# Where one Tanh stands in ScalarE's order, in a soft-capped attention fused with a spectral token mixer

## The chip, the core and the metric

The kernel runs on one core of a Trainium2 chip. The core has a TensorE (matmul, in the profile PE, with its weight loads PEld), a VectorE (DVE), a ScalarE (ACT), a GpSimd (POOL) and a SyncE (SP), which here issues nearly all DMAs. Each engine executes its own instructions in the order in which they were written for it, and waits on semaphores for the others. The metric is device time in microseconds (us) of one execution; of a kernel with several runs, the median.

## The reference

Batch 8, 12 heads, sequence 448, head size 64, model width 768. All in float32.

```python
def _attn_ref(q, k, v, cap):
    scores = np.matmul(q, k.transpose(0, 1, 3, 2)) / np.sqrt(q.shape[-1])
    scores = cap * np.tanh(scores / cap)
    scores = scores - np.max(scores, axis=-1, keepdims=True)
    attn = np.exp(scores)
    attn = attn / (np.sum(attn, axis=-1, keepdims=True) + 1e-09)
    return np.matmul(attn, v)

def _moe_ref(x, w_theta, w_tok_r, w_tok_i, w_ch):
    theta = x @ w_theta
    zr, zi = x * np.cos(theta), x * np.sin(theta)
    y = np.einsum('ts,bsd->btd', w_tok_r, zr) + np.einsum('ts,bsd->btd', w_tok_i, zi)
    u = x + y
    return u + np.maximum(u @ w_ch, 0.0)
```

The attention's output, with its heads side by side, is the `x` of the second function.

## The kernel before

Heads are worked in pairs: 8 batches of 6 pairs, 48 pairs in all. Activations lie transposed, with features in the partitions. float32 products whose accuracy matters are made of three matmuls on operands that are split into a rounded high part and a low remainder (`zh` and `zl`, `hi` and `lo`, `wtk_h` and `wtk_l`): high by high, high by low, low by high.

The function `pipeline` writes one slot after the other. Slot `s` makes the scores of pair `s` and, one slot late, the attention output of pair `k = s - 1`; from slot 8 on (FIRST) it also holds one sixth of the second function for batch `b`, called its part: `b, part = divmod(s - 8, 6)`. There are 56 slots, and slots from 48 on have no scores (`live` is false). What an engine does in which order is set by the order in which this Python code writes the instructions; no scheduler moves them.

A slot writes, in this order: the first half of the scores (`qk_half(s, 0)`: matmuls of line 217 into the PSUM tile `s`, then a Tanh of line 219 from there into the tile `p`); the attention output (`av`, line 257, and its copy `x` on ScalarE, line 260); the sums of the exponentials (`sums`, line 273, into the PSUM tile `r`); the second half of the scores with its Tanh (`qk_half(s, 1)`); then the list of steps of its part (`part_scripts`). In that list "A" and "B" stand for the Exp of the first and second half (line 225), "a" and "b" for partial sums of the exponentials on VectorE (lines 247 and 250).

The steps that this document speaks of:
- `transp(b, j)` (lines 355 to 357): seven transposes on TensorE of feature block `j` into two PSUM tiles `t`, four and three blocks. For each of the two, ScalarE rounds it to `zh` (line 356) and VectorE subtracts to get `zl` (line 357).
- `mix(b, j)` (lines 364 to 367): 21 matmuls of `zh` and `zl` with the token weights into a PSUM tile `mx`, then an addition to `x` on VectorE.
- `sincos` (lines 341 and 342): two Sin passes on ScalarE, with a table load ahead; the next Exp needs another load.
- `rotate` (line 346): x times sine and cosine, on VectorE.
- `invert` (line 296): the reciprocal `ri` of the sums `r` on VectorE, and four DMAs on SyncE that spread it to `bc`. It is written for odd `k` only.
- `prep(s + 1)` (lines 193 and 194): the split of the next pair's q and k on VectorE, from slot 13 on, and a DMA for the pair behind.

Part 2 of each batch is the slot whose list begins with a transposition, `(transp, 1)`; 1 is the feature block, the first one having been transposed at the end of part 1. Its list is transp 1, sincos 1, mix 0, rotate 3, transp 2, "A", mix 1, "a", rotate 4, transp 3, "B", mix 2, "b", rotate 5. Parts 2 with scores are slots 10, 16, 22, 28, 34, 40 and 46. In them `invert` and `prep` are written right behind the first entry, so VectorE takes the reciprocal after the two subtractions of transp 1.

PSUM has two pools. `psS` holds one tile `s`, which both halves of the scores use in turn. `psM` holds four tiles, shared by `a`, `r`, `t`, `th`, `mx` and `ch`: a new one takes the buffer that was released first in program order.

Of the kernel before, what the change touches and what calls it, by code (L numbers as in the profile page):

```python
# [16 lines left out]
AF = mybir.ActivationFunctionType  # L17
# [15 lines left out]
WHOLE = 14  # L33
# [3 lines left out]
def softcap_attn_then_spectral_mix(ctx, tc, qk2, v, cap, w_theta, w_tok, w_ch, ident, outT):  # L37
    nc = tc.nc
    B, NP, P, _, S = qk2.shape
    D = P // 2  # L40
    CP = v.shape[2]
# [4 lines left out]
    NS = B * NP  # L46
# [14 lines left out]
    qscale = const.tile([P, 1], F32, name="qscale")  # L61
# [20 lines left out]
    def fill(n):  # L82

        t = psM.tile([P, 512], F32, tag="m", name=f"fill{len(fills)}")
        fills.append(t)
        for _ in range(n):
            nc.tensor.matmul(t[:32, :CP], ones_sb, ones_sb[:, :1].broadcast_to([CP, CP]), start=True, stop=True)
# [77 lines left out]
    def weights(s, pos):  # L165
        for word in WEIGHTS.get((s, pos), "").split():
            step = steps[word[-3:-1], int(word[-1])]
            {">": step.load, "*": step.scale, "#": step.vscale}.get(word[0], step.split)()
# [8 lines left out]
    def load_qk(k):  # L177

        if 0 < k < WHOLE:
            raw[k] = wk.tile([P, 2, S], F32, tag=("hi", "lo")[k % 2], name=f"qk{k}", bufs=1)  # L180
        else:
            raw[k] = qk_sb
        nc.sync.dma_start(raw[k], qk2[k // NP, k % NP])

    def load_v(k):
        vt[k] = wk.tile([CP, 2, NCH, D], F32, tag="v", name=f"v{k}", bufs=2)
        nc.sync.dma_start(vt[k], v[k // NP, k % NP])
# [10 lines left out]
    def apart(k):  # L198


        return k < NP and k % 2 == 0

    def qk_half(k, half):

        sp = psS.tile([P, 2, 2, 512], F32, tag="s", name=f"s{k}_{half}")
        if apart(k):
            pp = wk.tile([CP, 2, 2, S], F32, tag="xhl", name=f"p{k}_{half}", bufs=3)
        else:
            pp = wk.tile([CP, 2, 2, S], F32, tag="p", name=f"p{k}_{half}", bufs=3)
        pt[k, half] = pp  # L210
        for i in range(2):
            ks = slice((2 * half + i) * CP, (2 * half + i + 1) * CP)
            products = ((raw, raw),) if k < WHOLE else ((hi, hi), (lo, hi), (hi, lo))
            for n, (kk, qq) in enumerate(products):
                for hh in range(2):
                    rows = slice(hh * D, (hh + 1) * D)
                    nc.tensor.matmul(sp[:CP, i, hh, :S], kk[k][rows, 1, ks], qq[k][rows, 0, :],  # L217
                                     start=n == 0, stop=n == len(products) - 1)
        nc.scalar.activation(pp, sp[:CP, :, :, :S], AF.Tanh, scale=qscale[:CP])  # L219

    def exp_half(k, half):

        pp = pt[k, half]
        if not state["general"]:
            nc.scalar.activation(pp, pp, AF.Exp, scale=cap_sb[:CP])  # L225
        elif half:
            first = pt[k, 0]
            mx = wk.tile([CP, 2, S], F32, tag="ps", name=f"mx{k}", bufs=2)
            am = wk.tile([CP, 2, S], F32, tag="ps", name=f"am{k}", bufs=2)
            nc.vector.tensor_tensor(mx, first[:, 0], first[:, 1], op=ALU.max)  # L230
            nc.vector.tensor_tensor(mx, mx, pp[:, 0], op=ALU.max)
            nc.vector.tensor_tensor(mx, mx, pp[:, 1], op=ALU.max)
            nc.gpsimd.partition_all_reduce(am, mx, CP, bass_isa.ReduceOp.max)
            for t in (first, pp):
                for i in range(2):
                    nc.vector.tensor_tensor(t[:, i], t[:, i], am, op=ALU.subtract)
                nc.scalar.activation(t, t, AF.Exp, scale=cap_sb[:CP])
# [14 lines left out]
    def av(k):  # L252
        va = vt.pop(k)
        acc = psM.tile([P, 512], F32, tag="m", name=f"a{k}")
        for c in range(NCH):
            for hh in range(2):
                nc.tensor.matmul(acc[hh * D : (hh + 1) * D, :S], va[:, hh, c, :], pt[k, c // 2][:, c % 2, hh, :],  # L257
                                 start=c == 0, stop=c == NCH - 1)
        x = wk.tile([P, S], F32, tag="x", name=f"x{k}", bufs=12)
        nc.scalar.copy(x, acc[:, :S])  # L260
        X[k // NP, k % NP] = x
# [13 lines left out]
    def sums(k, halves=(0, 1)):  # L275

        alone = state["general"] or NP <= k < DIRECT
        if not alone and k % 2 == 0:
            return
        if state["general"] and 0 not in halves:  # L280
            return
        if (k % 2 == 0 or not alone) and 0 in halves:
            state["r"] = psM.tile([P, 512], F32, tag="m", name=f"r{k}")
        sum_pairs((k,) if alone else (k - 1, k), state["r"], halves)

    def invert(k):

        if k % 2 == 0:
            return
        r = state.pop("r")  # L290
        ri = wk.tile([P, S], F32, tag="ri", name=f"ri{k}", bufs=1)
        if state["general"]:
            nc.vector.tensor_scalar_add(ri, r[:, :S], 1e-9)
            nc.vector.reciprocal(ri, ri)
        else:
            nc.vector.reciprocal(ri, r[:, :S])  # L296
        for n in (k - 1, k):
            bc[n] = wk.tile([P, S], F32, tag="bc", name=f"bc{n}", bufs=2)
            for i in range(2):
                nc.sync.dma_start(bc[n][i::2, :], ri[D * (n % 2) : D * (n % 2) + D, :])  # L300
# [92 lines left out]
    def us(b, j):  # L393
        split_x(b, j, "us")

    def pipeline(general):
        state["general"] = general
        load_v(0)
        load_qk(1)
        for step in (("tk", 0), ("tk", 1)):  # L400
            steps[step].load()

        for s in range(FIRST + 6 * B):
            k = s - 1
            b, part = divmod(s - FIRST, 6)
            live = s < NS
            start = s < FIRST
            if s == 0:
                fill(FILL["first scores"])
            if live:  # L410
                qk_half(s, 0)
            if s == 0:
                fill(FILL["half"])
            if start:
                weights(s, "a")
                exp_half(s, 0)
            if 0 <= k < NS:
                av(k)
            if not start:
                weights(s, "a")  # L420
            if not start and part == 4:
                for j in range(NJ // 2, NJ):
                    us(b, j)
            if s + 1 < NS:
                load_v(s + 1)
            if 0 <= k < NS:
                sums(k, (0,) if start else (0, 1))
                if not start and part != 2:
                    invert(k)
            if live:  # L430
                qk_half(s, 1)
            if s == 0:
                fill(FILL["slot"])
            if 0 <= k and start:
                sums(k, (1,))
            if s + 2 <= WHOLE:
                load_qk(s + 2)
            if WHOLE <= s + 1 < NS and (start or part != 2):
                prep(s + 1)
            weights(s, "b")  # L440
            if 0 <= k and start:
                invert(k)
            script = ["B", "a", "b"] if start else part_scripts(b)[part]
            for i, e in enumerate(script):
                if not start and i == len(script) - 1:
                    weights(s, "c")
                    if s % 2 == 1 and s <= NS + 1:
                        norm(s - 3)
                        norm(s - 2)
                if isinstance(e, str):  # L450
                    if live:
                        if e in "AB":
                            exp_half(s, "AB".index(e))
                        else:
                            add_half(s, "ab".index(e))
                else:
                    e[0](b, e[1])
                if part == 2 and i == 0 and not start:
                    if 0 <= k < NS:
                        invert(k)  # L460
                    if WHOLE <= s + 1 < NS:
                        prep(s + 1)
            if start:
                weights(s, "c")
                for n in {4: (0, 1), 5: (2, 3), 7: (4, 5)}.get(s, ()):
                    norm(n)
                for j in {6: range(4), 7: range(4, NJ)}.get(s, ()):
                    split_x(0, j, "xs")
# [12 lines left out]
    with arm.Else():  # L481
        with tc.manual_schedule():
            pipeline(general=True)
# [38 lines left out]
```

## Time and profile before

| | |
|---|---|
| median of 3 runs | 964.53 us (964.43 to 966.29) |
| profiled execution | 966.27 us |
| its span, first to last instruction | 964.5 us |
| granted TensorE clock, mean | 0.997 |
| Tanh (line 219), 96 times | 168.7 us, 1757 ns each |
| Exp (line 225), 96 times | 170.6 us, 1790 ns each |
| rounding of transposes (line 356), 96 times | 45.9 us, 534 ns mean of two shapes |
| subtraction (line 357), 96 times | 55.2 us, 616 ns mean of two shapes |
| reciprocal (line 296), 24 times | 70.8 us, 2952 ns each |
| table loads on ScalarE, 30 | 1283 ns each |

In a row of the timeline stand the start in us from the span's start, the duration in us, the engine, the line, the operation, the names (output, then inputs, without buffer numbers), the shapes and a count of instructions drawn together; in brackets the idle time of the engine ahead of it, and what ended it. Waits are inferred from semaphore events. A TensorE row's start is recorded, and its end is modelled.

### The profile page before, as it was taken

To read this page: it belongs to the slowest core of one execution; us is meant where nothing else is said; L and a number is where in the kernel's file an instruction comes from. 1 tells how busy PE (TensorE), PEld (TensorE's weight loads), DVE (VectorE), ACT (ScalarE), POOL (GpSimd) and SP (SyncE) were. 2 spreads that over 40 slices of the span, in tenths; PEclk is the share of its full clock that TensorE was granted. 3 is DMA by queue.
4 is the path that set the end of the run, shared out by engine and by line. 5 is a ranking of instruction groups with operands and counts; after the bars stand their busy time and mean duration, and the time that the engine had idled before them with its cause. 6 is when DMAs were issued, how large, how long until landed. Compare 5 with 4: busy or idle time off the path is not lost.

```text
span 964.5 us, 12776 instructions
## 1 busy us (share of the span) xinstructions
PE 945.6 (98%) x5224; PEld 697.3 (72%) x5224; DVE 640.8 (66%) x877; ACT 590.5 (61%) x609; POOL 0.4 (0%) x6
## 2 busy tenths in 40 slices
PE   8999999999999999999999999999999999999997
PEld 4234766677778777777787687767777877789897
DVE  5998787885855757756766559656585576664541
ACT  6888784667654687546963578456775558722520
POOL 0000000000000000000000000000000000000000
PEclk9999999999999999999999999999999999999999
DMA  7564122330113212132122221033011321001001
GB/s 252 193 194 138 34 82 94 112 103 30 49 39 105 67 39 63 32 98 67 32 66 68 77 67 48 29 87 94 31 49 39 105 68 39 20 15 62 0 1 61
DMA packets 30739, 68.68 MB, mean 71 GB/s; under 512 B 4304, under 2 KB 16720, under 8 KB 30672
## 3 DMA queue, kind: packets, MB, share of 16 engines
q1 hardware_dynamic: 30672, 67.78, 23.0%
q8 instruction: 43, 0.70, 0.3%
q14 instruction: 24, 0.20, 0.1%
HBM read 45.74 MB, written 11.01 MB: 59 GB/s over the span
## 4 chain that ended last, share of the span: by engine, by line
PE 88%; DVE 6%; ACT 4%; issue 1%; POOL 0%; POOLq 0%
PE a L257 15%; PE s L217 14%; PE mx L364 6%; PE mx L366 6%; PE mx L365 6%; PE th L322 6%; PE ch L322 6%; PE ch L324 6%; PE th L323 6%; PE ch L323 6%; PE th L324 6%; PE t L355 3%; PE r L273 3%; ACT p L219 2%; DVE ri L296 2%
## 5 line engine op out<-in xcount | busy, mean ns | idle before, releaser
L219 ACT ACTIVATE p<-s,qscale 112x1792 f32<-112x1792 f32 x96 | 168.7, 1757 | 168.7 <-PE s L217 168.7
L225 ACT ACTIVATE p<-p,cap_sb 112x1792 f32<-112x1792 f32 x96 | 170.6, 1790 | 0.6
L257 PE MATMUL a<-p,v 112*64 112x448 f32 x768 | 154.9, 545 | 0.0
L364 PE MATMUL mx<-wtk_h,zh 128*128 128x448 f32 x336 | 126.8, 377 | 5.4 <-DVE ri L296 3.6
L366 PE MATMUL mx<-wtk_h,zl 128*128 128x448 f32 x336 | 123.6, 368 | 0.0
L365 PE MATMUL mx<-wtk_l,zh 128*128 128x448 f32 x336 | 123.5, 367 | 0.0
L257 PEld LDWEIGHTS a<-p,v 112*64 112x64 f32 x768 | 50.9, 136 | 86.9 <-issue 77.1
L322 PE MATMUL th<-xs,wth_h 128*128 128x448 f32 x288 | 106.9, 371 | 0.0
L322 PE MATMUL ch<-us,wch_h 128*128 128x448 f32 x288 | 106.8, 371 | 0.0
L324 PE MATMUL ch<-us,wch_l 128*128 128x448 f32 x288 | 105.5, 366 | 0.0
L323 PE MATMUL th<-xs,wth_h 128*128 128x448 f32 x288 | 105.4, 366 | 0.0
L323 PE MATMUL ch<-us,wch_h 128*128 128x448 f32 x288 | 105.3, 366 | 0.0
L324 PE MATMUL th<-xs,wth_l 128*128 128x448 f32 x288 | 105.3, 366 | 0.0
L250 DVE TENSOR_TENSOR ps<-ps,p 112x896 f32<-112x896 f32 x80 | 87.0, 1087 | 1.4
L296 DVE RECIPROCAL ri<-r 128x448 f32<-128x448 f32 x24 | 70.8, 2952 | 12.0 <-PE r L273 11.9
L335 DVE SCALAR_TENSOR_TENSOR g_sb<-g_sb 128x448 f32<-128x448 f32 x48 | 29.9, 624 | 65.8 <-ACT g_sb L334 65.4
L364 PEld LDWEIGHTS mx<-wtk_h,zh 128*128 128x128 f32 x336 | 63.6, 189 | 11.9 <-issue 5.0
L357 DVE TENSOR_TENSOR zl<-t,zh 128x512 fp32r<-128x512 f32 x96 | 55.2, 616 | 24.5 <-ACT zh L356 24.5
L375 DVE SCALAR_TENSOR_TENSOR x<-ch,x 128x448 f32<-128x448 f32 x48 | 29.8, 620 | 59.0 <-PE ch L324 59.0
L366 PEld LDWEIGHTS mx<-wtk_h,zl 128*128 128x128 f32 x336 | 63.5, 189 | 5.4
L365 PEld LDWEIGHTS mx<-wtk_l,zh 128*128 128x128 f32 x336 | 63.7, 190 | 4.9
L322 PEld LDWEIGHTS ch<-us,wch_h 128*128 128x128 f32 x288 | 54.1, 188 | 9.6 <-issue 4.6
(75 smaller groups left out, 1377.8 us busy)
## 6 DMA issues: line engine op xcount, KB each, us to landing
qk_sb<-in_qk SPq DMA_DIRECT2D x35, 448.0 KB, 3.4
v<-in_v SPq DMA_DIRECT2D x48, 224.0 KB, 2.5
bc<-ri SPq DMA_DIRECT2D x96, 112.0 KB, 2.3
out_dram<-x SPq DMA_DIRECT2D x48, 224.0 KB, 1.9
qk<-in_qk SPq DMA_DIRECT2D x13, 448.0 KB, 3.4
g_sb<-in_wth SPq DMA_DIRECT2D x6, 768.0 KB, 5.4
g_sb<-in_wch SPq DMA_DIRECT2D x6, 768.0 KB, 4.7
swk_raw<-in_wtok SPq DMA_DIRECT2D x7, 448.0 KB, 4.1
```

The lines of the kernel that those rows point to most:

```text
L217: nc.tensor.matmul(sp[:CP, i, hh, :S], kk[k][rows, 1, ks], qq[k][rows, 0, :], start=n == 0, stop=n == len(products) - 1)
L219: nc.scalar.activation(pp, sp[:CP, :, :, :S], AF.Tanh, scale=qscale[:CP])
L225: nc.scalar.activation(pp, pp, AF.Exp, scale=cap_sb[:CP])
L250: nc.vector.tensor_tensor(pst[k], pst[k], pt[k, 1][:, i], op=ALU.add)
L257: nc.tensor.matmul(acc[hh * D : (hh + 1) * D, :S], va[:, hh, c, :], pt[k, c // 2][:, c % 2, hh, :], start=c == 0, stop=c == NCH - 1)
L296: nc.vector.reciprocal(ri, r[:, :S])
L322: nc.tensor.matmul(acc[:, :S], wh[:, j, ms], t[:, 0, :], start=j == 0, stop=False)
L323: nc.tensor.matmul(acc[:, :S], wh[:, j, ms], t[:, 1, :], start=False, stop=False)
L324: nc.tensor.matmul(acc[:, :S], wl[:, j, ms], t[:, 0, :], start=False, stop=j == NJ - 1)
L364: nc.tensor.matmul(acc[:, :S], zh[:, c, :], wtk_h[:, c, :], start=c == 0, stop=False)
L365: nc.tensor.matmul(acc[:, :S], zh[:, c, :], wtk_l[:, c, :], start=False, stop=False)
L366: nc.tensor.matmul(acc[:, :S], zl[:, c, :], wtk_h[:, c, :], start=False, stop=c == NC2 - 1)
```

## The change

`qk_half` no longer issues its Tanh; it returns a function that does. For the first half, and for the second half of every slot but the parts 2, that function is called at once, so nothing moves there. In the parts 2 (`late`) it is called after the first entry of the list, that is after `transp(b, 1)`, ahead of `invert` and `prep`, which stand where they stood.

```diff
-        nc.scalar.activation(pp, sp[:CP, :, :, :S], AF.Tanh, scale=qscale[:CP])
+        return lambda: nc.scalar.activation(pp, sp[:CP, :, :, :S], AF.Tanh, scale=qscale[:CP])
...
             if live:
-                qk_half(s, 0)
+                qk_half(s, 0)()
...
+            late = not start and part == 2
             if live:
-                qk_half(s, 1)
+                tanh = qk_half(s, 1)
+                if not late:
+                    tanh()
...
-            if WHOLE <= s + 1 < NS and (start or part != 2):
+            if WHOLE <= s + 1 < NS and (not late):
                 prep(s + 1)
...
-                if part == 2 and i == 0 and not start:
+                if late and i == 0:
+                    if live:
+                        tanh()
                     if 0 <= k < NS:
                         invert(k)
                     if WHOLE <= s + 1 < NS:
```

ScalarE's instructions in slot 22 (batch 2), before and after; the number behind a name tells instances apart, `p_1` is the second half of the scores, and `zh_1` the rounding of transp 1:

```order
 L219 ACTIVATE p_0_2664<-s_0_2663,qscale 112x1792
 L260 COPY x_2687<-a_2678 128x448
+L356 CAST zh_1_2710<-t_1_0_2712 128x512
+L356 CAST zh_1_2710<-t_1_4_2719 128x384
 L219 ACTIVATE p_1_2697<-s_1_2696,qscale 112x1792
-L356 CAST zh_1_2711<-t_1_0_2713 128x512
-L356 CAST zh_1_2711<-t_1_4_2720 128x384
 L341 ACT_TABLE_LOAD
 L341 ACTIVATE g_sb_87<-g_sb_87,quarter 128x3x448
```

The two roundings have passed the Tanh; the same happens in the six other slots. No table load is added.

VectorE's instructions at the same place, which are the same in both kernels but for the instance numbers (those of before are shown), with the engines that each waits for:

```order
L357 TENSOR_TENSOR zl_1_2712<-t_1_0_2713,zh_1_2711 128x512 [waits Activation_49]
L357 TENSOR_TENSOR zl_1_2712<-t_1_4_2720,zh_1_2711 128x384 [waits Activation_49]
L296 RECIPROCAL ri_2726<-r_2691 128x448
L193 CAST hi_2734<-qk_sb 128x896 [waits DMAHW7_49]
L194 TENSOR_TENSOR lo_2735<-qk_sb,hi_2734 128x896 [waits DVE_49]
L367 TENSOR_TENSOR x_1359<-mx_0_2741,x_1359 128x448 [waits PE_49]
L346 TENSOR_TENSOR g_sb_87<-g_sb_87,x_1780 128x896 [waits Activation_49]
```

Nothing has moved on VectorE: the reciprocal still stands behind the two subtractions, and these wait for ScalarE.

TensorE's instructions from transp 2 to the start of mix 1 in that slot, again the same in both:

```order
L355 MATMUL t_2_0_2767<-ident_sb,g_sb_86 128x128 [waits DVE_49]
L355 MATMUL t_2_0_2767<-ident_sb,g_sb_86 128x128 x3
L355 MATMUL t_2_4_2774<-ident_sb,g_sb_86 128x128 [waits DVE_49]
L355 MATMUL t_2_4_2774<-ident_sb,g_sb_86 128x128 x2
L364 MATMUL mx_1_2781<-wtk_h,zh_1_2711 128x448 [waits DVE_49,Activation_49]
```

Nothing has moved here either: the first matmul of mix 1 waits for VectorE and for ScalarE.

## The prediction

> **What bounds the kernel now.** I read the page first: busy shares, then the chain that ended last.
>
> ```profile
> PE 945.6 (98%) x5224; PEld 697.3 (72%) x5224; DVE 640.8 (66%) x877; ACT 590.5 (61%) x609; POOL 0.4 (0%) x6
> PE 88%; DVE 6%; ACT 4%; issue 1%; POOL 0%; POOLq 0%
> ```
>
> TensorE is busy 98% of the span and carries 88% of the chain. A reordering on ScalarE can only buy what TensorE waits for. So the next view is the list of TensorE's waits (us in total, times, longest):
>
> ```profile
> PE s L217 <- ACT p L219: 6.7, 7, 1.9
> PE mx L364 <- DVE ri L296: 3.6, 7, 0.5
> ```
>
> The second row matters: seven times a mix matmul (line 364) waits for VectorE's reciprocal `ri`. Seven is the number of slots that the change touches (s = 10, 16, 22, 28, 34, 40, 46), and 3.6/7 = 0.51 us each, with a longest of 0.5, so they are alike. The first row is the second scores' wait for the first half's Tanh, which the change leaves in place. The timeline of slot 22, rows of three engines in order of time (start, duration), shows what stands behind such a wait:
>
> ```profile
> 359.76 0.98 PE L355 MATMUL t<-ident_sb,g_sb 128*128 128x128 f32 x7
> 359.86 1.76 ACT L219 ACTIVATE p<-s,qscale 112x1792 f32<-112x1792 f32 x1 [1.76 <-PE s L217]
> 360.00 1.08 DVE L346 TENSOR_TENSOR g_sb<-g_sb,x 128x896 f32<-128x896 f32 x1
> 361.52 0.95 ACT L356 CAST zh<-t 128x512 fp32r<-128x512 f32 x2
> 362.13 1.16 DVE L357 TENSOR_TENSOR zl<-t,zh 128x512 fp32r<-128x512 f32 x2 [1.05 <-ACT zh L356]
> 362.49 1.28 ACT L341 ACT_TABLE_LOAD   x1
> 363.20 2.94 DVE L296 RECIPROCAL ri<-r 128x448 f32<-128x448 f32 x1
> 364.65 0.37 PE L366 MATMUL mx<-wtk_h,zl 128*128 128x448 f32 x1
> 364.86 0.93 PE L355 MATMUL t<-ident_sb,g_sb 128*128 128x128 f32 x7
> 365.11 1.31 ACT L342 ACTIVATE g_sb<-g_sb 128x1344 f32<-128x1344 f32 x1
> 366.29 0.45 PE L364 MATMUL mx<-wtk_h,zh 128*128 128x448 f32 x1 [0.51 <-DVE ri L296]
> 366.32 0.94 ACT L356 CAST zh<-t 128x512 fp32r<-128x512 f32 x2
> 368.20 1.08 DVE L346 TENSOR_TENSOR g_sb<-g_sb,x 128x896 f32<-128x896 f32 x1
> 368.58 1.80 ACT L225 ACTIVATE p<-p,cap_sb 112x1792 f32<-112x1792 f32 x1
> 369.20 1.15 DVE L357 TENSOR_TENSOR zl<-t,zh 128x512 fp32r<-128x512 f32 x2
> 370.44 0.37 PE L366 MATMUL mx<-wtk_h,zl 128*128 128x448 f32 x1
> 370.65 0.93 PE L355 MATMUL t<-ident_sb,g_sb 128*128 128x128 f32 x7
> 371.29 0.97 ACT L356 CAST zh<-t 128x512 fp32r<-128x512 f32 x2 [0.91 <-PE t L355]
> 371.33 0.45 PE L364 MATMUL mx<-wtk_h,zh 128*128 128x448 f32 x1
> 371.39 1.08 DVE L247 TENSOR_TENSOR ps<-p 112x896 f32<-112x896 f32 x1
> 372.14 1.81 ACT L225 ACTIVATE p<-p,cap_sb 112x1792 f32<-112x1792 f32 x1
> ```
>
> Read backwards: mix 1 starts at 366.29, 0.15 after the reciprocal ends (363.20 + 2.94 = 366.14), because it takes the PSUM buffer that `r` leaves. The reciprocal stands behind the two subtractions `zl` in VectorE's queue. These waited 1.05 us for the rounding `zh` on ScalarE, and `zh` stood behind the Tanh of 359.86. The transposes that `zh` reads had begun at 359.76. So the Tanh is in the way of a chain that ends in a TensorE wait.
>
> **What the wait costs.** Its printed length is 0.51, but that counts from a modelled end of the transposes. I use starts. With the wait, from the last matmul of a mix to the first of the next: 364.65 to 366.29, 1.64 us. Without it, after the next transposes: 370.44 to 371.33, 0.89 us. The difference is **0.75 us** a slot. [...]
>
> **Part 1: `zh` ahead of the Tanh.** Where ScalarE is already idle, `zh` starts 371.29 - 370.65 = 0.64 after its transposes. So here it starts at 359.76 + 0.64 = 360.40, 1.12 earlier. The subtraction follows 0.61 later (362.13 - 361.52): 361.01. VectorE is free by then: an instruction after a rotation (line 346) starts 1.00 after it (368.20 to 369.20), so from 361.00. The reciprocal follows 1.07 later (362.13 to 363.20), at 362.08, ends at 365.02, and mix 1 may start at 365.17. TensorE itself is ready 0.68 after the transposes (370.65 to 371.33), at 365.54. The wait is gone with 0.37 to spare, and the slot gains its full 0.75.
>
> Slot 10 is tighter, since VectorE's rotation comes later against the transposes there:
>
> ```profile
> 128.44 0.98 PE L355 MATMUL t<-ident_sb,g_sb 128*128 128x128 f32 x7
> 128.56 1.76 ACT L219 ACTIVATE p<-s,qscale 112x1792 f32<-112x1792 f32 x1 [1.73 <-PE s L217]
> 129.26 1.08 DVE L346 TENSOR_TENSOR g_sb<-g_sb,x 128x896 f32<-128x896 f32 x1
> 130.82 1.16 DVE L357 TENSOR_TENSOR zl<-t,zh 128x512 fp32r<-128x512 f32 x2 [0.48 <-ACT zh L356]
> 134.99 0.44 PE L364 MATMUL mx<-wtk_h,zh 128*128 128x448 f32 x1 [0.52 <-DVE ri L296]
> ```
>
> `zh` could start at 129.08 and `zl` at 129.69, but the rotation holds VectorE until 130.26 (129.26 + 1.00). So `zl` moves from 130.82 by 0.56 and mix 1 with it; 0.2 us of a wait stays.
>
> **Part 2: what the Tanh's new place delays.** Tanh and rounding together took ScalarE from 359.86 to the table load at 362.49. Now they begin at 360.40, with `zh` 0.85 long to the next start (371.29 to 372.14), so the Tanh starts at 361.25. How long a Tanh holds up a table load is in slot 15:
>
> ```profile
> 226.32 1.77 ACT L219 ACTIVATE p<-s,qscale 112x1792 f32<-112x1792 f32 x1 [0.86 <-PE s L217]
> 228.11 1.28 ACT L341 ACT_TABLE_LOAD   x1
> ```
>
> That is 1.79, so the load starts at 363.04, 0.55 late, and so does all behind it on ScalarE. Queued there: both Sin passes, the second rounding, a table load, Exp of half one, the third rounding, Exp of half two. Who waits for them:
> - The rotation of 368.20 needs the sines, which end at 365.11 + 1.31 + 0.55 = 366.97. VectorE would reach it at 368.20 - 1.12 = 367.08. Covered by 0.1; the cover behind it is larger: `zl` of the second transposes starts 1.00 later and ends at 369.23, and mix 2 starts at 371.33 - 0.75 = 370.58. So 1.35 us less 0.15 of signalling is the slack.
> - The second rounding moves to 366.87, ahead of that `zl`.
> - The Exp of half one ends at 368.58 + 1.80 + 0.55 = 370.93. The third rounding, possible from 369.90 + 0.64 = 370.54, then starts 0.4 late, and the partial sum (line 247) about as late. The third rounding's user, mix 3, belongs to the next slot, after mix 2 and all its scores. The Exp of half two starts at 371.8 instead of 372.14: not late.
>
> Nothing else moves: the reciprocal's DMAs of `bc` and the split of the next q and k come up to 1.1 us earlier on their queues, and no wait is added to TensorE or VectorE. The Tanh's own scores buffer is next written at the following slot's start, behind the whole of mix 2.
>
> **Part 3: contention.** Tanh and VectorE's reads of PSUM now run together. The nearest rows are these, starting at the same time:
>
> ```profile
> 173.14 1.76 ACT L219 ACTIVATE p<-s,qscale 112x1792 f32<-112x1792 f32 x1 [0.71 <-PE s L217]
> 173.14 2.95 DVE L296 RECIPROCAL ri<-r 128x448 f32<-128x448 f32 x1
> ```
>
> Both have the length that they have elsewhere (1.76 and 2.94 in slot 22), so I charge 0. No instruction is dropped, so there is no gain to bound from below; from above, up to 0.37 a slot would vanish in the spare of part 1.
>
> [...] The table load now follows a Tanh where it followed a rounding. The row of 228.11 starts 0.02 after its Tanh's end, so here no extra time stands between. [...]
>
> **The sum.** Six slots at 0.75 and one at 0.56: 4.5 + 0.56 = **5.06 us**. Behind slot 10 TensorE stays the clock of the rest, by its 98%. The profiled execution took 966.27 with a span of 964.5; it becomes 961.2 and 959.4. It lies 1.74 above the median of the three runs, 964.53, and near their highest, 966.29. From the median: 964.53 - 5.06 = **959.5**.
>
> **Rivals.**
> - *Only part of it comes.* If `zh` starts 0.6 late (waiting for all seven transposes, which take 0.98 by 359.76), or if the printed idle time is the true prize, 3.6 to 3.7 us are left: 960.9. For it: rounding directly behind transposes that follow scores does not occur in these rows. Against: the 0.64 of 371.29.
> - *Nothing changes.* Mix 1 would wait for something else that ends when the reciprocal does: 964.5. Against it: the start 0.15 after `ri`, and `zl` waiting for `zh`. For it: the profile names only the last releaser, and the wait row has two semaphores.
> - *Slower, by a turn of table loads.* If Tanh behind the rounding drew one more pair of loads, 2 x 1.28 = 2.57, ScalarE would be 0.55 + 2.57 = 3.12 late. The sines end at 369.54, `zl` at 371.69, mix 2 starts at 371.84, that is 0.51 behind the present 371.33. Over seven slots that is 3.6 us: 968.1. It loses from a delay of about 2.6 us on. Against it: no load is added in ScalarE's order.
>
> **How the numbers follow.** Full gain 0.64 (959.5; up to 961.2 where a run lies as high as the profiled one), part 0.18 (960.9), nothing 0.11, slower 0.07. The range 958.6 to 963.0 holds the first two, with that spread of 1.7 on either, and leaves out 0.18. A measurement of this kernel tells about 0.2%, 1.9 us, from no change: faster 0.82, same 0.11, slower 0.07.
>
> **What would show it.** After the change, TensorE's wait for `ri` is gone, by starts but for about 0.2 us in slot 10; in slot 22 `zh` starts about 0.64 after the transposes, the reciprocal 1.1 earlier, ScalarE's table load 0.55 later; mix 2 waits for nothing. I am wrong if mix 1 still starts 1.4 after its transposes, or if a new wait for `zl` or the rotated `g_sb` appears at mix 2 or at the third transposes.

## The result and the profile after

| | before | after |
|---|---|---|
| median of 6 runs each | 966.21 us (964.43 to 966.55) | 959.97 us (957.74 to 960.93) |
| profiled execution | 966.27 | 959.56 |
| its span | 964.5 | 957.8 |
| mean granted TensorE clock | 0.997 | 0.999 |

The ratio after to before is 0.9939, with a 95% interval of 0.9926 to 0.9951. The forecast was 959.5, in a range of 958.6 to 963.0.

The page of after, busy shares and chain (engines, with shares of the span):

```profile
PE 942.3 (98%) x5224; PEld 696.3 (73%) x5224; DVE 641.6 (67%) x877; ACT 589.8 (62%) x609; POOL 0.4 (0%) x6
PE 93%; ACT 3%; DVE 3%; issue 1%; POOL 0%; POOLq 0%
```

VectorE's share of the chain has halved, from 6% to 3%. TensorE's waits in after (us in total, times, longest):

```profile
PE s L217 <- ACT p L219: 6.7, 7, 1.9
PE mx L364 <- DVE zl L357: 1.8, 1, 1.8
```

The seven waits for `ri` are gone from this list, and no wait has come in their place. The two rows that are left were there before, unchanged. The timeline of slot 22 in after, three engines in order of time:

```profile
358.30 0.98 PE L355 MATMUL t<-ident_sb,g_sb 128*128 128x128 f32 x7
358.54 1.08 DVE L346 TENSOR_TENSOR g_sb<-g_sb,x 128x896 f32<-128x896 f32 x1
359.00 0.97 ACT L356 CAST zh<-t 128x512 fp32r<-128x512 f32 x2 [2.35 <-PE t L355]
359.62 1.15 DVE L357 TENSOR_TENSOR zl<-t,zh 128x512 fp32r<-128x512 f32 x2
359.85 1.77 ACT L219 ACTIVATE p<-s,qscale 112x1792 f32<-112x1792 f32 x1
360.69 2.95 DVE L296 RECIPROCAL ri<-r 128x448 f32<-128x448 f32 x1
361.63 1.28 ACT L341 ACT_TABLE_LOAD   x1
362.93 1.42 ACT L341 ACTIVATE g_sb<-g_sb,quarter 128x1344 f32<-128x1344 f32 x1
363.20 0.37 PE L366 MATMUL mx<-wtk_h,zl 128*128 128x448 f32 x1
363.40 0.93 PE L355 MATMUL t<-ident_sb,g_sb 128*128 128x128 f32 x7
364.09 0.45 PE L364 MATMUL mx<-wtk_h,zh 128*128 128x448 f32 x1
364.25 1.31 ACT L342 ACTIVATE g_sb<-g_sb 128x1344 f32<-128x1344 f32 x1
365.69 1.08 DVE L346 TENSOR_TENSOR g_sb<-g_sb,x 128x896 f32<-128x896 f32 x1
366.69 1.15 DVE L357 TENSOR_TENSOR zl<-t,zh 128x512 fp32r<-128x512 f32 x2
368.45 0.93 PE L355 MATMUL t<-ident_sb,g_sb 128*128 128x128 f32 x7
369.13 0.45 PE L364 MATMUL mx<-wtk_h,zh 128*128 128x448 f32 x1
369.43 0.94 ACT L356 CAST zh<-t 128x512 fp32r<-128x512 f32 x2
```

The rounding now starts 0.70 behind its transposes (359.00 - 358.30; before 1.76). The reciprocal starts 2.39 behind them (before 3.44). Mix 1 follows the last matmul of mix 0 by 0.89 (363.20 to 364.09), where it took 1.64.

Slot 10, the tight one, in after:

```profile
129.13 1.08 DVE L346 TENSOR_TENSOR g_sb<-g_sb,x 128x896 f32<-128x896 f32 x1
130.14 1.15 DVE L357 TENSOR_TENSOR zl<-t,zh 128x512 fp32r<-128x512 f32 x2
131.20 2.94 DVE L296 RECIPROCAL ri<-r 128x448 f32<-128x448 f32 x1
133.21 0.37 PE L366 MATMUL mx<-wtk_h,zl 128*128 128x448 f32 x1
134.29 0.45 PE L364 MATMUL mx<-wtk_h,zh 128*128 128x448 f32 x1
```

The subtractions start 1.01 behind VectorE's rotation, and mix 1 starts 0.15 after the reciprocal's end and 1.08 behind the last matmul of mix 0 (133.21 to 134.29). Against the 0.89 of slot 22, 0.19 us of the wait is left by starts, though the list above has no row for it.

**Where the time went.** ScalarE's copies of the attention outputs are marks that both kernels have, one for each pair. That of pair 47, the last:

```profile
858.38 0.53 ACT L260 COPY x<-a 128x448 f32<-128x448 f32 x1 [9.45 <-PE a L257]
```

```profile
853.09 0.53 ACT L260 COPY x<-a 128x448 f32<-128x448 f32 x1 [9.45 <-PE a L257]
```

The first is of before, the second of after. (A pair's copy is made one slot after its scores; the expectations below call this mark the copy of slot 47.) Distances between marks, worked out from such rows:

| from the copy of pair | to that of pair | what lies between | before | after | less by |
|---|---|---|---|---|---|
| start of span | 0 | start | 20.13 | 20.01 | 0.12 |
| 9 | 10 | transposes of slot 10 | 23.16 | 22.59 | 0.57 |
| 15 | 16 | slot 16 | 22.89 | 22.16 | 0.73 |
| 21 | 22 | slot 22 | 22.90 | 22.15 | 0.75 |
| 27 | 28 | slot 28 | 22.90 | 22.16 | 0.74 |
| 33 | 34 | slot 34 | 22.90 | 22.16 | 0.74 |
| 39 | 40 | slot 40 | 22.96 | 22.16 | 0.80 |
| 45 | 46 | slot 46 | 22.90 | 22.16 | 0.74 |
| 0 | 47 | all that the change touches | 838.25 | 833.08 | 5.17 |
| 47 | end of span | last batch, no scores | 106.12 | 104.71 | 1.41 |

Of the 6.70 us between the two spans, 5.17 come from the stretch with the seven slots, 5.07 of it within those slots, and 1.41 from the tail (from the copy of pair 47 to the end), where the two kernels have the same instructions in the same order. The tail's cause is in the granted clock. Three windows behind TensorE's wait in slot 52 (us, busy time of each engine with its instructions, then PEclk, DMA share, GB/s), in before:

```profile
906.00:908.00 2.00, 1.17 (x5) 1.08 (x6) 2.00 (x4) 2.00 (x4) 0.00 (x0) 0.89 0.00 0
908.00:910.00 2.00, 2.00 (x7) 1.78 (x6) 1.30 (x3) 0.91 (x1) 0.00 (x0) 0.50 0.00 0
910.00:912.00 2.00, 2.00 (x9) 1.80 (x9) 0.00 (x0) 0.00 (x0) 0.00 (x0) 0.75 0.00 0
```

and in after, the same three behind the same wait:

```profile
900.70:902.70 2.00, 1.15 (x6) 1.08 (x7) 2.00 (x4) 2.00 (x4) 0.00 (x0) 1.00 0.00 0
902.70:904.70 2.00, 2.00 (x11) 1.84 (x10) 1.32 (x3) 0.94 (x1) 0.00 (x0) 1.00 0.00 0
904.70:906.70 2.00, 2.00 (x15) 1.85 (x14) 0.57 (x2) 0.14 (x1) 0.00 (x0) 1.00 0.00 0
```

In before the clock falls to half for 3.4 us; in after it does not.

### The profile page after: what moved, and what is told of

It reads as the page before. It is cut to its first block, busy times and chain, and to the rows that moved or that the text cites. A ratio compares the mean times of both kernels' runs of the same rounds, so it can differ in the third digit from the quotient of the medians.

```text
span 957.8 us, 12769 instructions
## 1 busy us (share of the span) xinstructions
PE 942.3 (98%) x5224; PEld 696.3 (73%) x5224; DVE 641.6 (67%) x877; ACT 589.8 (62%) x609; POOL 0.4 (0%) x6
## 4 chain that ended last, share of the span: by engine, by line
PE 93%; ACT 3%; DVE 3%; issue 1%; POOL 0%; POOLq 0%
PE a L257 15%; PE s L217 14%; PE mx L364 7%; PE mx L366 7%; PE mx L365 7%; PE th L322 6%; PE ch L322 6%; PE ch L324 6%; PE th L324 6%; PE th L323 6%; PE ch L323 6%; PE t L355 4%; PE r L273 3%; ACT p L219 2%; PE fill L87 1%
## 5 line engine op out<-in xcount | busy, mean ns | idle before, releaser
L356 ACT CAST zh<-t 128x512 fp32r<-128x512 f32 x96 | 45.8, 532 | 31.1 <-PE t L355 31.1
```

## The experiments

Times are medians against the runs of before in the same comparison; "ratio" is with its 95% interval. Gains are by the marks, from the copy of pair 0 to that of pair 47, so they hold neither the start nor the tail.

**One: three of the seven slots.** From after:

```diff
-                if not late:
+                if not late or b % 2 == 0:
                     tanh()
...
-                    if live:
+                    if live and b % 2 == 1:
                         tanh()
```

> The Tanh goes behind the rounding in slots 16, 28 and 40 only. Theory (each slot gives its own 0.75 us by starts): 3 x 0.75 = 2.25 us less than before, so ScalarE's copy of the attention output in slot 47, which stood at 858.38 before and at 853.09 after, stands at 856.1, and TensorE's wait for the reciprocal is left in four slots. Rival (the printed idle time of 0.51 a slot is the true prize): 1.5 us, copy at 856.9. Rival (the gain is not in these slots, but comes from TensorE's clock near the end): copy at 858.4.

Measured: 962.4 us, ratio 0.9965 (0.9952 to 0.9977). Slots 16, 28 and 40 give 0.74, 0.74 and 0.80, and the other four lie within 0.02 of before; the total is 2.33. The wait for `ri` is left four times. The rival that counted printed idle time (1.5) and the one that saw no gain in the slots both fall. The mark itself stands at 854.0 instead of 856.1, for this profiled execution was 2.0 ahead at the copy of pair 0 already. That is the start: the first scores took 1.76 us here and 3.33 in before (TensorE rows of this kernel, then of before):

```profile
5.23 1.76 PE L217 MATMUL s<-qk_sb 64*112 64x448 f32 x8 [0.16 <-DMA qk_sb<-in_qk]
```

```profile
5.36 3.33 PE L217 MATMUL s<-qk_sb 64*112 64x448 f32 x8
```

The trace's record of the granted clock begins, at full clock, at 4.48 us in this kernel and at 9.87 in before. In the traces of all twelve kernels it begins either at 4.3 to 4.5 us (four of them, with the copy of pair 0 at 18.1 to 18.2) or at 9.0 to 10.5 (eight, with that copy at 19.8 to 20.5). The windows ahead of it print 1.00 too (before: 0 to 4, 4 to 8 and 8 to 9.86), so the mean clock does not show the start. So there are two places where runs of one kernel part: the start, by some 2 us, and slot 52. Hence the marks.

**Two: the reciprocal first, the Tanh where it was.** From before:

```diff
-                if not start and part != 2:
+                if not start:
                     invert(k)
...
                 if part == 2 and i == 0 and not start:
-                    if 0 <= k < NS:
-                        invert(k)
```

> The order of before, with the Tanh ahead of the rounding; instead the reciprocal is written ahead of the first transposes' subtractions on VectorE in the slots that begin with transposes. Theory (mix 1 waits only for the buffer that the reciprocal frees, and what stands ahead of the reciprocal does not matter): the reciprocal starts 1.0 after the rotation, ends before the transposes of mix 1 are through, and the subtractions behind it are in time: 0.75 us in six slots and about 0.6 in slot 10, 5.1 us in all, copy of slot 47 at 853.2, time as after. Rival (the Tanh itself was in the way, on ScalarE or in PSUM): nothing, copy at 858.4.

Measured: 959.53 us, ratio 0.9935 (0.9918 to 0.9953), gain 5.27: 0.69 in slot 10 and 0.73 to 0.80 in the six others. Slot 22 of this kernel:

```profile
359.79 2.95 DVE L296 RECIPROCAL ri<-r 128x448 f32<-128x448 f32 x1
362.65 1.09 DVE L357 TENSOR_TENSOR zl<-t,zh 128x512 fp32r<-128x512 f32 x2
363.64 0.93 PE L355 MATMUL t<-ident_sb,g_sb 128*128 128x128 f32 x7
364.32 0.45 PE L364 MATMUL mx<-wtk_h,zh 128*128 128x448 f32 x1
```

The subtractions wait for the reciprocal here, and mix 1 starts 0.68 behind its transposes all the same. The Tanh has not moved, so it was never in the way by itself; it was ahead of the one thing that mix 1 waits for.

**Three and four: the Tanh twice, in the old place and in the new.** The second Tanh writes the values of the first again. Three, from before:

```diff
-        nc.scalar.activation(pp, sp[:CP, :, :, :S], AF.Tanh, scale=qscale[:CP])
+        for _ in range(times):        # times is a new argument, 1 by default
+            nc.scalar.activation(pp, sp[:CP, :, :, :S], AF.Tanh, scale=qscale[:CP])
...
-                qk_half(s, 1)
+                qk_half(s, 1, 2 if not start and part == 2 else 1)
```

Four, from after:

```diff
                     if live:
                         tanh()
+                        tanh()
```

> The order of before, with the Tanh of the second half done twice in the slots that begin with transposes (the second one writes the same values again). Theory (all of the Tanh stands in the chain to mix 1): 1.66 us more in each of seven slots, 11.6 us, copy of slot 47 at 870.0, time 977.8, and TensorE's wait for the reciprocal 2.2 us each. Rival (the Tanh is only partly in the chain, another path takes over): clearly less than 11.6.

> The order of after, with the same Tanh done twice, both behind the rounding. Theory (ScalarE's delay meets a slack of about 1.2 us before mix 2, by way of the sines, the rotation and the second subtractions): 1.66 us more on ScalarE costs 0.4 us a slot at mix 2, 2.9 us in all, copy of slot 47 at 856.0, time 962.9. Rival (no slack, the new place is as tight as the old one): 11.6 us. Rival (the delay never reaches TensorE): 0, copy at 853.1.

Measured, in the old place: 978.5 us, ratio 1.0141 (1.0118 to 1.0165). TensorE's seven waits for `ri` take 2.3 us each, where 2.2 was expected. Five slots lose 1.73 to 1.80 us each, and slots 16 and 28 lose 3.3 to 3.4. A Tanh behind a Tanh takes 1.78 to the next start, not the 1.66 that I had used, and the two costly slots have the clock at half behind the wait, as these windows of slot 16 show, PEclk being the third number from the end:

```profile
252.00:254.00 2.00, 0.83 (x3) 0.80 (x4) 1.97 (x3) 2.00 (x4) 0.00 (x0) 0.86 0.00 0
254.00:256.00 2.00, 2.00 (x7) 1.78 (x6) 2.00 (x3) 1.97 (x3) 0.00 (x0) 0.50 0.76 170
256.00:258.00 2.00, 2.00 (x9) 1.80 (x9) 1.23 (x3) 1.25 (x1) 0.00 (x0) 0.79 0.84 262
```

So all of the Tanh stands in the chain there, as the theory has it, and the excess of the total (15.5 instead of 11.6) is 0.9 from the length and about 3 from the clock. The median rose by 12.2 only, because the runs of before mostly have the late start and the fall in the tail, and the profiled run of this kernel has neither; that 978.5 lies near the expected 977.8 is luck.

In the new place: 963.05 us, ratio 0.997 (0.9958 to 0.9981). By the marks it gains 1.90 against before, so the second Tanh costs 5.17 - 1.90 = 3.27, or 0.47 a slot (0.48 to 0.50 in six, 0.30 in slot 10), where 0.4 was expected. Slot 22 of this kernel:

```profile
367.28 1.31 ACT L342 ACTIVATE g_sb<-g_sb 128x1344 f32<-128x1344 f32 x1
368.62 1.09 DVE L346 TENSOR_TENSOR g_sb<-g_sb,x 128x896 f32<-128x896 f32 x1 [1.61 <-ACT g_sb L342]
369.63 1.15 DVE L357 TENSOR_TENSOR zl<-t,zh 128x512 fp32r<-128x512 f32 x2
370.84 0.47 PE L364 MATMUL mx<-wtk_h,zh 128*128 128x448 f32 x1
```

The rotation waits 1.61 for the sines, the subtractions follow it, and mix 2 starts as they end. That is the next chain in line, in the place where the prediction had it. The same 1.78 us of ScalarE cost 1.78 in the old place and 0.47 in the new.

**Five to eight: the wait in slot 52.** Small matmuls into an unused PSUM tile fill TensorE's wait, in the order of before and in that of after:

```diff
+    def keep_busy(n):
+        t = psS.tile([P, 2, 2, 512], F32, tag="s", name="busy")
+        for _ in range(n):
+            nc.tensor.matmul(t[:32, 0, 0, :CP], ones_sb, ones_sb[:, :1].broadcast_to([CP, CP]), start=True, stop=True)
...
+                    if not live:        # part 2, behind the first entry: slot 52
+                        keep_busy(16)   # later 8
```

> The order of after, and in slot 52 (the last batch's, without scores) 16 small matmuls into an unused PSUM tile between the transposes and mix 0, where TensorE otherwise waits 1.83 us for the subtractions. Theory (that wait lets the granted clock fall to half for some 3 us in some runs, which is why the runs of after lie apart): no run with a mean clock of 0.997, time about 959.8, and from the copy of slot 47 to the span's end 104.7. Rival (the runs lie apart for another reason): runs near 960.9 remain.

> The order of before, with the same 16 small matmuls in slot 52. Theory (in before the clock falls behind that wait, and this makes 1.4 us of the difference between before and after that is none of the moved Tanh's): time 964.8, mean clock 0.999, copy of slot 47 unchanged at 858.4 (0.3 more or less by the start), from there to the end 104.7 instead of 106.1. Rival (the tail is longer in before for a reason of the change itself): 966.2 and 106.1.

Measured: 960.03 us, ratio 0.9942 (0.9929 to 0.9955), for after with 16; 965.94, ratio 1.0001 (0.9992 to 1.0009), for before with 16. The times say little, since my dose was wrong: the 16 matmuls are 32 instructions and take 3.3 us, and mix 0 came late. Three of the six runs of after with 16 stay near 961 (960.97 to 961.35), as the rival had it; but their mean clock is 1.0, so it is the start, not slot 52, that holds them 2 us above the other three. The clock did not fall in either profiled execution, and the tails are 105.95 and 105.95: equal, where they had been 104.71 and 106.12. So with half the dose:

> The order of before with 8 small matmuls in slot 52 instead of 16 (16 took 3.3 us, as 32 instructions, where the wait was 1.83, and put mix 0 off by 1.3). Theory (the clock falls behind the wait, and 1.4 us of the difference between before and after is that): the 8 take 1.65 us and fit in, from the copy of slot 47 to the end 104.7 instead of 106.1, time 964.9, no clock of 0.997. Rival (the shorter tail of after belongs to its order): 106.1 and 966.3.

> The order of after with 8 small matmuls in slot 52. Theory: from the copy of slot 47 to the end 104.7 as in the profiled run of after, time 959.7, and against the run before this one 5.2 us, which is what the seven slots give. Rival: some other difference than 5.2 between the two.

Measured: 964.65 for before with 8, ratio 0.9991 (0.9982 to 1.0), and 959.63 for after with 8, ratio 0.9941 (0.9928 to 0.9954). The filling and the start of mix 0, in the first:

```profile
902.75 1.75 PE L95 MATMUL busy<-ones_sb 112*32 112x112 f32 x16
904.65 0.47 PE L370 MATMUL mx<-wtk_h,zh 128*128 128x448 f32 x1 [0.15 <-DVE zl L363]
```

The tails are 104.61 and 104.68: that of before has become as short as that of after. With the clock's fall taken out, the two orders lie 964.65 - 959.63 = 5.0 us apart by their medians and 5.02 by their marks, which is what the slots give. None of 12 and 5 runs had a mean clock of 0.997. In this comparison the median of before itself was 964.61, since more of its runs had the clock at 0.999 or the early start; so the single ratio of this pair to before shows nothing, and the tails do.

**Nine and ten: taking that wait away.** For the last batch, the transposes' rounding and subtraction are written ahead of what follows the sixth angle block:

```diff
+    def theta_transp(b, j, i):
+        acc = proj(b, wth_h, wth_l, j, "th")
+        transp(b, i)
+        phase(b, j, acc)            # ScalarE and VectorE work of theta, taken out of it
...
-            "B", "b", (theta, 5), (transp, 0), (rotate, 2)],
+            "B", "b"] + ([(lambda b, j: theta_transp(b, j, 0), 5)] if b == B - 1
+                         else [(theta, 5), (transp, 0)]) + [(rotate, 2)],
```

> The order of after; in the last batch, which has no scores between the parts, ScalarE and VectorE take the rounding and the subtractions of the first transposes ahead of the work behind the sixth angle block, instead of behind it. Theory (the wait of 1.83 us in slot 52 stands behind that work on both engines): rounding 0.6 and subtraction 1.5 earlier, the wait is 0.3, from the copy of slot 47 to the end 103.2, time 958.4, and no run with a clock of 0.997. Rival (the work that is put back is then waited for in its turn, at the second sines): as after, 959.9.

> The order of before with the reciprocal ahead of the subtractions (as in the second experiment) and the last batch's rounding first (as in the run before this one). If the two add up: the second experiment's 959.5 less 1.5, 958.0, copy of slot 47 at 853.2 and 103.2 from there to the end.

Measured: 958.27 us (958.14 to 958.58), ratio 0.9922 (0.9909 to 0.9935), on the order of after; 958.07 (957.91 to 958.85), ratio 0.9921 (0.9908 to 0.9933), on that of the second experiment. The tails are 103.45 and 103.47, 1.25 less than in after, where 1.5 was expected. A row of the first one's waits has the difference:

```profile
PE t L357 <- ACT g_sb L335: 0.7, 1, 0.7
```

The transposes now wait for the PSUM buffer of the angle block whose reading was put back. The rival had this wait at the second sines. ScalarE does wait there, 0.70 us for the work that was put back, but TensorE waits for it only at the transposes. By medians and tails both are faster than before and after; the one from the other cannot be told.

## Why the prediction was right

- **What mix 1 waits for.** Right. Experiment two moved only `invert`, the reciprocal with its DMAs, and gained the same.
- **The price of the wait, 0.75 by starts.** Right: 0.73 to 0.80 in six slots. By printed idle time it would have been 0.51. Experiment one, with its three slots, shows the same.
- **Slot 10, 0.56.** Right: 0.57, and of the 0.2 of a wait that was to stay, 0.19 stays by starts. That VectorE's rotation is the limit there is in the rows of slot 10 and agrees with experiment two, where the reciprocal comes directly behind that rotation and the slot gives 0.69.
- **The delay on ScalarE.** The table load was to come 0.55 later; against the transposes it came 0.60 later (3.33 behind them instead of 2.73). The third rounding was to start 0.4 late; it starts 0.98 behind its transposes instead of 0.64, so 0.34 late. Nothing of it reached TensorE, and experiment four found the slack where it had been placed, before mix 2, at 1.78 - 0.47 = 1.3.
- **No price for contention and none for the table load behind a Tanh.** Right: the Tanh has 1.77 in slot 22 of after, the reciprocal 2.95, the subtractions 1.15, the load starts 0.01 after the Tanh's end, and the Sin behind it 0.02 after the load's.
- **The sum.** The stretch that the change touches gave 5.17, for 5.06. The step that was incomplete is the one that went from the sum to a span, "Behind slot 10 TensorE stays the clock of the rest, by its 98%": it let the tail stand at the length that the profiled execution of before had. That tail held 1.41 us of half clock, which after mostly does not have, so the span came out at 957.8, not 959.4. I had also put down the 1.74 between the profiled execution and the median as a spread without asking where it arises: at the start (about 2 us) and in slot 52 (1.4). That the median landed so near the forecast, 959.97 for 959.5, is in part luck: the forecast started from 964.53, where the median of before is 966.21 over all six runs. Between the medians lie 6.24 us, of which the stretch with the slots gives 5.17; the rest is, as far as the traces show, the start and the clock in slot 52.

Why the clock falls behind that wait in most runs of before and in few of after is open; no run was made to test it. The wait is 1.83 us in both profiles. In the comparison with experiments five, six, nine and ten, 4 of 17 runs of before had 0.999 and took 964.4 to 964.6; of the others, 11 took 966.2 to 966.8 and two 964.3 to 964.4. Of the six runs of after, two had 0.997, at 960.75 and 960.93.

The clock records of the traces hold a lead. In all twelve, every change of the clock comes a whole number of times 3.413 us after the first full clock. In before that is at 9.87, and the fall comes 263 such steps later, at 907.58, and lasts one step. In after it is at 9.61, and the one change comes 277 steps later, at 955.10. Windows of before that are cut at these edges:

```profile
904.16:907.58 3.42, 1.59 (x12) 1.30 (x11) 2.82 (x6) 3.42 (x7) 0.00 (x0) 1.00 0.00 0
907.58:910.99 3.41, 3.41 (x11) 3.02 (x10) 1.72 (x3) 1.33 (x2) 0.00 (x0) 0.50 0.00 0
910.99:914.40 3.41, 3.41 (x22) 3.17 (x21) 1.45 (x2) 0.97 (x2) 0.00 (x0) 1.00 0.00 0
```

The whole wait of before lies in the first of these windows. In after an edge at 900.48 cuts the same wait, and its longer piece is 1.06 us. The traces have thirteen such waits, those of slot 52 in six kernels and the seven of experiment three. The three that a fall follows have 1.83, 2.14 and 2.31 us between two edges; the ten others have 1.73 at most. That is not the whole rule: in its first slots each kernel waits 1.85 us for a Tanh three times, 23 of these 36 waits lie whole between two edges, and no fall follows them.

## What to carry to other kernels

Follow a TensorE wait back through the queues of the engines, not through the data: here a Tanh that nothing waited for stood ahead of a rounding, that ahead of a reciprocal, and the reciprocal held a PSUM buffer. Price such a wait by the starts of the instructions on both sides, against the same pair without a wait, and check the slack of what is put back, for it is the next limit. And before two kernels are compared to a tenth of a percent, compare them stretch by stretch with marks that both have, for the rest of the program may differ by the clock alone, as the tails of before and after do here, by 1.41 us.

## What the runs showed of the hardware

A single wait of TensorE of 1.83 us, behind 64 us in which TensorE was busy without a gap (64.00 from 840 to 904), was followed in the trace of before by 3.41 us at half the granted clock, which cost 1.4 us more than the wait (tails of 106.12 and 104.71); 36 of the 46 runs of before in the three comparisons had the same mean clock, 0.997. Waits of 2.3 us in experiment three did it in two of seven slots, at some 1.6 us there. Filled with small matmuls, the same place left no such fall in any of the four profiled executions. In all twelve traces the clock changed only in whole steps of 3.413 us from its first full moment (263, 264 and 279 steps in before, 277 in after), and of the thirteen late waits those with a fall behind them had the longest pieces between two edges of these steps: 1.83, 2.14 and 2.31 us, against 1.73 at most. The steps begin at another moment in each trace (9.87 us in before, 9.61 in after, 4.48 in experiment one). How long a wait is enough was not shown: of the 36 waits of 1.85 us in the first slots, 23 lie whole between two edges, and no fall follows them.
